# A fused attention and FFN kernel: the order of work from a table of places instead of shifts

## The chip, the core and the metric

One NeuronCore of a Trainium2 chip runs the kernel. Times are microseconds of device time of an execution; the median of the runs counts. The engines are TensorE (PE, matmuls; PEld is its weight load), VectorE (DVE), ScalarE (ACT), GpSimd (POOL), and SyncE (SP), which issues every DMA of this kernel.

## What is computed

Four batches of eight heads, 576 rows of 64 columns, go through causal attention and a memory retrieval, mixed by a gate; the result, as 2304 tokens of 512, goes through a feed-forward layer of 2048 with its own negative slope for each hidden unit:

```python
scores = scale * np.matmul(q, k.transpose(0, 1, 3, 2))
scores = np.where(causal, -1000000000.0, scores)
a = np.exp(scores - scores.max(-1, keepdims=True))
a /= a.sum(-1, keepdims=True) + 1e-09
local = np.matmul(a, v)
q_p = phi(q)                                   # elu(q) + 1
mem_out = einsum(q_p, M_prev) / (einsum(q_p, z_prev) + 1e-06)
x = g * mem_out + (1 - g) * local              # g = sigmoid(beta), per head
h = x @ w_in                                   # 2304 x 512 by 512 x 2048
y = (np.maximum(h, 0.0) + alpha * np.minimum(h, 0.0)) @ w_out
```

The two weight matrices arrive as 64-bit floats. The kernel reads them as pairs of 32-bit integers and puts fp32 together on DVE.

## The kernel before

The rows are cut so that each batch has 64 first rows and four blocks of 128. The 64 first rows of all four batches make a group of their own, `Z`, which comes first; then each batch goes in two halves (blocks 1 and 2, blocks 3 and 4), and each half is a group of 256 tokens for the feed-forward layer. Attention, the retrieval and the layer's two matmuls of different groups overlap.

The names that matter in the trace: `R` are the weights (and the first rows' k and v before them); `kn` and `E` also hold weight pieces at the start. `q`, `kn`, `vn` and `zb` are loads. `s`, `s2` are scores in PSUM, `P` the probabilities, `PT` the turned ones (a DMA turns them), `bank` the product of `PT` and `v`, `xn` the scaled result, `x` the turned `xn`. `h` is the layer's first product, `gg` its activated value in two fp16 parts, `y` the second product, `t` the rows to store. `qT`, `k` and `qS` (a copy of `qT` with its halves swapped) feed the scores. `gco`, `igc`, `iom` are made from beta, `oma`, `ast`, `scd` and `scr` from alpha.

Nothing of this is issued where it is written. Every call on an engine goes through `Work.add`, which records the operation, what it depends on and a price from `Work.price`. `Work.phase` names each one's stage: `LW0` to `LW3` are loads of weight pieces, `C0` to `C3` their conversion (`to_f32`, three DVE operations of 128x1024 for a piece, whose data come in two loads), `J` the small constants, `sZ` and `oZ` the first rows' scores and values, `s21`, `P21`, `o21` scores, probabilities and values of batch 2's first half, `h1_11` and `y1_11` the two products of batch 1's first group, its second four steps, and so on. At the end `Work.issue` puts all 6253 operations (4158 of PE, 1053 of DVE, 626 of ACT, 138 of POOL, 278 DMAs) into one order, and the engines run theirs in it; only data and buffers hold an instruction back. All of them stand in the trace under the line that issues them, L487.

`lay` makes the order: a list scheduler with one clock for each engine, that takes of the operations that are ready the one with the lowest rank. In the kernel before, ranks begin as latest start times. `STAGES` then shifts all operations of a stage, or of a stage on one engine, by one number, and passes forwards and backwards follow, stage after stage of the table:

```python
rank = [x + 1e3 * sum(bias.get(k, 0) for k in ...) for x, op in zip(rank, ops)]
start = self.lay(before, after, rank)
```

So two operations of one stage on one engine keep the distance that the latest start times gave them, unless `lay` itself parts them.

Of the kernel before, what the change touches and what calls it, by code (L numbers as in the profile page):

```python
# [31 lines left out]
STAGES = [  # L32
    (2, {
        "A0": 10.6, "A:DVE": 50.6, "BK0": 102.5, "BK:ACT": -27.7, "BK:PE": 3.4, "C0": -56.4, "C1": 22.3, "C2": 335.8,
        "C3": -920, "C:ACT": 1096.2, "C:DVE": -3.8, "C:PE": -943.6, "I": -699.2, "I:DVE": 79.2, "I:POOL": 497.7,
        "J:ACT": 470.6, "J:DVE": 108, "J:PE": -179.3, "K": 47.5, "K:POOL": 2.3, "L0K": -713.8, "L0K:DMA": 228.2,
# [6 lines left out]
        "LW:DMA": 605.3, "LZ": 27.3, "LZ:DMA": -1145.9, "Lz": 8.5, "Lz:DMA": -8.6, "N": 87.9, "N:PE": 292.5,  # L43
        "P01": 4, "P03": 3.7, "P11": 777.2, "P13": 823.4, "P21": 168.1, "P23": 236.6, "P31": -675.3, "P33": -247.2,
        "P:ACT": 988.7, "P:DMA": 668.5, "P:DVE": -882.6, "P:PE": -157.8, "S0": 4737.2, "S1": -1253, "S3": -2953.6,
        "S:ACT": -87.5, "S:DVE": 168.1, "V0": -874.8, "V:DVE": 211.2, "V:PE": -90.8, "a0": 5.7, "a1": 46.8,
        "a2": -161.5, "a3": 389.6, "a4": -42.9, "a:ACT": -265.2, "a:DVE": 239.4, "bk0": -173.5, "bk1": 344.8,
        "bk2": 244.5, "bk3": 3.1, "bk:ACT": -687.5, "bk:DMA": 246.9, "bk:DVE": 1380.7, "bk:PE": 100.3, "bv0": -0.7,
# [1479 lines left out]
```

## Time and profile before

| | us |
|---|---|
| median of 3 runs | 562.34 |
| the runs | 561.42 to 563.78 |
| the profiled execution | 563.66 |
| its span | 561.9 |

The span is what the views below divide; 1.76 us of the profiled execution lie outside it. Idle time in a view of one engine stands in brackets at the end of a row, with what released the engine. A DMA's row on SP is its issue, the landing comes later. PE's weight loads run beside its matmuls, and the start of one matmul to the start of the next, not its own duration, is what it costs.

### The profile page before, as it was taken

What the parts mean: (1) busy time and instruction counts of PE and PEld (TensorE: products, weight loads), DVE (VectorE), ACT (ScalarE), POOL (GpSimd) and SP (SyncE); (2) the same over time, 40 slices, a digit from 0 to 9 for tenths busy, and PEclk for the clock granted to TensorE, in tenths of its full rate; (3) what the DMA queues carried; (4) which work ended last, traced back from release to release, by engine and by line L of the source; (5) the groups of instructions that cost most, each with busy time, mean ns of one, the idle gap of its engine ahead of it and who ended that gap; (6) DMA issues with size and microseconds to landing.
All of it is one profiled execution on the core that took longest, in us unless ns stands there. A gap on an engine that the chain in (4) does not pass through costs nothing. (4 is left out here: it accounts for less than half of the span.)

```text
span 561.9 us, 11984 instructions
## 1 busy us (share of the span) xinstructions
PE 536.4 (95%) x4421; PEld 353.5 (63%) x4421; DVE 450.9 (80%) x1197; ACT 376.7 (67%) x790; POOL 82.8 (15%) x142
## 2 busy tenths in 40 slices
PE   9749999999999899999998999999999999999997
PEld 3448654556557566658555766578578765866663
DVE  4989999999999799999897999998679974233232
ACT  2568996778998369978785787796579873232222
POOL 3000510031220012221222110431112110000000
PEclk9869999999999999999998999999999999999999
DMA  8998595836359997579999816799446963000000
GB/s 283 239 353 202 155 238 173 244 94 153 89 127 184 214 231 170 101 140 210 194 201 198 175 34 146 160 232 178 58 118 111 167 138 88 12 11 2 37 1 37
DMA packets 226026, 82.84 MB, mean 147 GB/s; under 512 B 216224, under 2 KB 216240, under 8 KB 225968
## 3 DMA queue, kind: packets, MB, share of 16 engines
q1 hardware_dynamic: 225968, 82.09, 64.5%
q8 instruction: 34, 0.56, 0.4%
q14 instruction: 24, 0.20, 0.1%
HBM read 35.66 MB, written 5.77 MB: 74 GB/s over the span
## 5 line engine op out<-in xcount | busy, mean ns | idle before, releaser
L487 PE MATMUL h<-x,R 128*128 128x256 f16 x1536 | 246.7, 273 | 1.9 <-DMA x<-xn 1.4
L487 PE MATMUL y<-R,gg 128*128 128x512 f16 (+1 forms) x832 | 247.0, 399 | 0.8 <-ACT k L487 0.6
L487 PE MATMUL bank<-v,PT 128*128 128x64 f16 x1224 | 182.1, 193 | 5.3 <-DMA PT<-P 4.5
L487 PEld LDWEIGHTS <-R 128*128 128x128 f16 x1536 | 148.6, 98 | 36.9 <-issue 6.5
L487 PEld LDWEIGHTS <-gg 128*128 128x128 f16 x768 | 74.4, 98 | 78.3 <-DVE gg L487 1.8
L487 PEld LDWEIGHTS <-PT 128*128 128x128 f16 x1224 | 114.4, 98 | 13.6 <-DMA PT<-P 6.9
L487 POOL TENSOR_SCALAR E<-q,nrm,sm 128x64 f32<-128x64 f32 x112 | 67.9, 618 | 310.9 <-DVE sm L487 269.8
L487 ACT ACTIVATE E<-E,mx 128x320 f32<-128x320 f32 (+3 forms) x136 | 81.1, 602 | 21.5 <-DVE mx L487 17.4
L487 DVE SCALAR_TENSOR_TENSOR P<-E,mx,P 128x384 f16<-128x384 f32 (+2 forms) x112 | 75.3, 699 | 8.5 <-ACT P L487 8.4
L487 ACT ACTIVATE P<-E,mx 128x384 f16<-128x384 f32 (+2 forms) x112 | 71.0, 675 | 15.8 <-POOL E L487 12.0
L487 DVE SCALAR_TENSOR_TENSOR r<-r,oma,h 128x256 f32<-128x256 f32 x128 | 56.6, 475 | 20.2 <-ACT r L487 20.0
L487 DVE SCALAR_TENSOR_TENSOR gg<-r,gsc,gg 128x512 f16<-128x512 f32 x56 | 41.8, 748 | 36.5 <-ACT gg L487 35.0
L487 ACT ACTIVATE r<-h 128x512 f32<-128x512 f32 x72 | 42.3, 589 | 35.8 <-PE h L487 23.9
L487 ACT ACTIVATE gg<-r,gsc 128x512 f16<-128x512 f32 x56 | 40.1, 717 | 37.4 <-PE y L487 33.4
L487 DVE CUSTOM_DVE_ANT_0 E<-s,mask,pm 128x320 f32<-128x320 f32 (+2 forms) x96 | 56.9, 608 | 7.6 <-PE s L487 7.5
L487 PE MATMUL s<-k,qT 128*128 128x64 f16 (+5 forms) x136 | 37.9, 294 | 1.3 <-DMA k<-k 1.3
L487 PE MATMUL s<-k,qS 128*128 128x192 f16 (+4 forms) x120 | 34.0, 294 | 0.0
L487 PE MATMUL h<-R 128*128 128x256 f32 x128 | 32.7, 383 | 0.0
L487 PEld LDWEIGHTS h<-R 128*128 128x128 f32 x128 | 22.3, 192 | 6.6 <-issue 3.0
L487 ACT ACTIVATION_READ_ACCUMULATOR E<-E,mx 128x1 f32 x124 | 23.5, 189 | 0.0
L487 ACT ACTIVATE xn<-bank,xsc 128x256 f16<-128x256 f32 x28 | 12.9, 462 | 12.3 <-PE bank L487 12.3
L487 DVE SCALAR_TENSOR_TENSOR xn<-bank,xsc,xn 128x256 f16<-128x256 f32 x28 | 13.4, 480 | 9.4 <-ACT xn L487 9.4
(183 smaller groups left out, 636.7 us busy)
## 6 DMA issues: line engine op xcount, KB each, us to landing
q<-in_q_dram SPq DMA_DIRECT2D x16, 256.0 KB, 4.3
vn<-in_v_dram SPq DMA_DIRECT2D x16, 256.0 KB, 5.2
out_dram<-t SPq DMA_DIRECT2D x16, 256.0 KB, 2.4
kn<-in_moe_w_in_dram SPq DMA_DIRECT2D x6, 512.0 KB, 6.7
kn<-in_moe_w_out_dram SPq DMA_DIRECT2D x6, 512.0 KB, 5.3
kn<-in_k_dram SPq DMA_DIRECT2D x12, 256.0 KB, 4.0
qS<-qT SPq DMA_DIRECT2D x24, 128.0 KB, 2.6
R<-in_moe_w_in_dram SPq DMA_DIRECT2D x4, 512.0 KB, 5.6
```

The costliest lines, as they stand in the source:

```text
L487: fn(*a, **kw)
```

## The change

`STAGES`, with its passes and shifts, goes. `PLAN` takes its place: for each stage on each engine a string of steps, one for each operation (`*n` repeats one), whose running sum, times 100, is the rank of that operation. `issue` makes a single pass of `lay` with these ranks. The prices of DMAs in `price` change as well. Operations, their data, tiles, buffers and dependencies are the same in both kernels; the recording line moves from L487 to L750.

```diff
-STAGES = [
-    (2, {
-        "A0": 10.6, "A:DVE": 50.6, "BK0": 102.5, "BK:ACT": -27.7, "BK:PE": 3.4, "C0": -56.4, "C1": 22.3, "C2": 335.8,
...
+PLAN = {
+    "J:DVE": "-904 -12 133 -418 41 302 131 -23 130 -170 6 -430 573 -88",
+    "LW0:DMA": "-1100 449 -440 244 189 169 -485 666",
...
             if "transpose" in name:
-                return (800 + 1.75 * kb if kb > 400 else 1130 + 0.6 * kb), 190 + 3.45 * kb, 1655, -1
+                return (800 + 1.75 * kb, 4.1 * kb, 1700, -1) if kb > 400 else (1130 + 0.6 * kb, 3.78 * kb, 1885, -1)
...
             if run >= 4096:
-                return 400, (2.75 if self.phase in ("LW0", "LW1") else 4.9) * kb, 2000, packets
+                rate, late = {"LW0": (3.2, 2600), "LW1": (2.7, 2450)}.get(self.phase, (3.55, 2150))
+                return 400, rate * kb, late, packets
             if run >= 512:
-                return 540, max(300, 4.06 * kb), 1800, packets
-            return 620, (273 if kb > 200 else 200) + 4.17 * kb, 2100, packets
+                if o.tensor.name in self.fixed:
+                    return 400, 1.4 * kb, 1950, packets
+                return (560, 5.3 * kb, 1765, packets) if kb < 200 else (530, 4 * kb, 1800, packets)
+            return (600, 4.5 * kb, 2050, packets) if kb > 200 else (620, 6 * kb, 2090, packets)
...
-        rank = late
-        for passes, bias in STAGES:
-            rank = [x + 1e3 * sum(bias.get(k, 0) for k in dict.fromkeys((
...
+        plan = {}
+        for x, steps in PLAN.items():
+            at, ranks = 0, []
+            for step, _, times in (y.partition("*") for y in steps.split()):
+                for _ in range(int(times or 1)):
+                    at += int(step)
+                    ranks.append(100.0 * at)
+            plan[x] = iter(ranks)
+        start = self.lay(before, after, [next(plan[f"{op[7]}:{op[0]}"]) for op in ops])
```

What that does to the rows is seen at two places. The first is the start. SP's first rows before:

```order
L487 DMA R<-in_moe_w_in_dram 128x1024 x4
L487 DMA kn_90<-in_moe_w_in_dram 128x1024
L487 DMA xn_103<-in_moe_alpha_dram 16x128
L487 DMA q_1_94<-in_z_prev_dram 64x512 x4
L487 DMA kn_90<-in_moe_w_in_dram 128x1024
L487 DMA gco<-in_beta_dram 128x8
L487 DMA E_0_92<-in_moe_w_in_dram 128x1024 x2
L487 DMA q_0_93<-in_q_dram 64x8x64
```

and SP's first rows now:

```order
L750 DMA R<-in_moe_w_in_dram 128x1024 x2
L750 DMA E_0_92<-in_moe_w_in_dram 128x1024
L750 DMA R<-in_moe_w_in_dram 128x1024
L750 DMA kn_90<-in_moe_w_in_dram 128x1024
L750 DMA R<-in_moe_w_in_dram 128x1024
L750 DMA gco<-in_beta_dram 128x8
L750 DMA q_1_94<-in_z_prev_dram 64x512
L750 DMA kn_90<-in_moe_w_in_dram 128x1024
L750 DMA q_1_94<-in_z_prev_dram 64x512 x2
L750 DMA xn_103<-in_moe_alpha_dram 16x128
```

The two loads of a piece of weights stood next to one another for the first pieces; now the loads of four pieces are interleaved, gco is the seventh instead of the twelfth and alpha (to `xn`) the twelfth instead of the sixth. DVE's first conversions, in rows with the semaphores that they wait for (DMAHW0 to 7 go to the loads in turn, so that DMAHW1 and DMAHW3 are the second and the fourth), before:

```order
L487 TENSOR_SCALAR R<-R 128x1024 [waits DMAHW1_49,DMAHW0_49]
L487 SCALAR_TENSOR_TENSOR R<-R 128x1024 [waits DVE_49] x2
L487 TENSOR_SCALAR R<-R 128x1024 [waits DMAHW3_49,DMAHW2_49]
L487 SCALAR_TENSOR_TENSOR R<-R 128x1024 [waits DVE_49]
L487 TENSOR_REDUCE ast_89<-bank_67 128x1 [waits PE_49]
L487 TENSOR_SCALAR oma<-bank_67 128x16
L487 SCALAR_TENSOR_TENSOR R<-R 128x1024 [waits DVE_49]
```

and now:

```order
L750 TENSOR_SCALAR R<-R 128x1024 [waits DMAHW3_49,DMAHW1_49]
L750 SCALAR_TENSOR_TENSOR R<-R 128x1024 [waits DVE_49] x2
L750 TENSOR_SCALAR igc<-igc 128x8 [waits Activation_49]
L750 TENSOR_SCALAR R<-R 128x1024 [waits DMAHW5_49,DMAHW0_49]
L750 RECIPROCAL iom<-igc 128x8 [waits DVE_49]
L750 SCALAR_TENSOR_TENSOR R<-R 128x1024 [waits DVE_49]
L750 TENSOR_SCALAR iom<-iom 128x8 [waits DVE_49]
```

The first conversion waits for later loads than before, the chain from beta (igc, iom) stands between the first conversions, and that from alpha (ast, oma) comes after them.

The second place is where batch 1's layer and batch 2's attention overlap. SP's rows there, from the transposes of batch 1's last probabilities to those of batch 2's first (the first two `PT` that are 10 blocks wide), before:

```order
L487 DMA_TRANSPOSE PT_116<-P_100 128x18x128
L487 DMA qS<-qT 64x1024 x2
L487 DMA_TRANSPOSE k_65<-k_0_101 128x10x128
L487 DMA out_dram<-t_1_118 128x512
L487 DMA_TRANSPOSE PT_113<-P_99 128x18x128
L487 DMA_TRANSPOSE k_65<-k_1_102 128x10x128
L487 DMA_TRANSPOSE PT_114<-P_100 128x18x128
L487 DMA_TRANSPOSE x_111<-xn_104 128x4x128
L487 DMA q_1_94<-in_q_dram 128x8x64 x2
L487 DMA kn_90<-in_k_dram 128x8x64 x2
L487 DMA_TRANSPOSE PT_115<-P_99 128x10x128
L487 DMA_TRANSPOSE PT_116<-P_100 128x10x128
```

and now:

```order
L750 DMA qS<-qT 64x1024 x2
L750 DMA_TRANSPOSE x_111<-xn_103 128x4x128
L750 DMA_TRANSPOSE PT_116<-P_100 128x18x128
L750 DMA_TRANSPOSE k_65<-k_0_101 128x10x128
L750 DMA q_1_94<-in_q_dram 128x8x64 x2
L750 DMA_TRANSPOSE PT_113<-P_99 128x18x128
L750 DMA_TRANSPOSE PT_114<-P_100 128x18x128
L750 DMA kn_90<-in_k_dram 128x8x64 x2
L750 DMA_TRANSPOSE k_65<-k_1_102 128x10x128
L750 DMA_TRANSPOSE x_111<-xn_104 128x4x128
L750 DMA_TRANSPOSE PT_115<-P_99 128x10x128
L750 DMA_TRANSPOSE PT_116<-P_100 128x10x128
```

The copies to `qS` (and the store, which is now further ahead) come before the wide `PT_116`, the q loads before the wide `PT_113`, and a `k` and an `x` transpose stand where q and kn loads stood ahead of the narrow `PT_115`. PE's rows around the first matmul that reads this `PT_115`, before:

```order
L487 MATMUL h_123<-x_110,R 128x256
L487 LDWEIGHTS R
L487 MATMUL h_124<-x_111,R 128x256
L487 LDWEIGHTS PT_115
L487 MATMUL bank_67<-v_66,PT_115 128x64
L487 LDWEIGHTS R
L487 MATMUL h_124<-x_111,R 128x256
```

and now:

```order
L750 MATMUL h_123<-x_111,R 128x256
L750 LDWEIGHTS gg_150
L750 MATMUL y_131<-R,gg_150 128x512
L750 LDWEIGHTS PT_115
L750 MATMUL bank_67<-v_66,PT_115 128x64
L750 LDWEIGHTS gg_150
L750 MATMUL y_131<-R,gg_150 128x512
```

The matmuls of the group on `x_110` are all done by then in the new order, and the `h` and `y` of the next group, on `x_111`, stand further on.

## Rows read from the trace of the kernel before

**Rows 1.** The page, busy time, share and instructions of each engine.

```profile
PE 536.4 (95%) x4421; PEld 353.5 (63%) x4421; DVE 450.9 (80%) x1197; ACT 376.7 (67%) x790; POOL 82.8 (15%) x142
```

**Rows 2.** Stretches: length, busy time by engine, granted clock (PEclk), DMA share, GB/s.

```profile
20.00:40.00 20.00, 9.98 (x84) 7.54 (x85) 18.17 (x79) 13.96 (x48) 0.00 (x0) 0.69 1.15 304
47.00:299.00 252.00, 244.99 (x1902) 158.14 (x1901) 240.77 (x641) 200.37 (x417) 45.69 (x71) 1.00 0.76 175
299.00:303.00 4.00, 1.35 (x15) 0.98 (x13) 2.16 (x6) 1.60 (x4) 1.69 (x2) 1.00 0.97 129
303.00:310.00 7.00, 7.00 (x49) 4.15 (x48) 5.35 (x15) 4.05 (x10) 0.77 (x2) 0.76 0.93 199
310.00:470.00 160.00, 159.41 (x1549) 110.34 (x1547) 138.16 (x375) 122.45 (x259) 30.36 (x54) 1.00 0.68 137
470.00:556.00 86.00, 86.00 (x670) 57.62 (x669) 27.21 (x53) 23.69 (x37) 0.00 (x0) 1.00 0.05 16
```

**Rows 3.** Timeline of PE: start, duration, operation, [idle before <- releaser].

```profile
39.43 1.51 PE L487 MATMUL h<-ident,P 128*128 128x128 f32 x6 [2.83 <-DVE P L487]
```

**Rows 4.** Timeline of DVE, 6 to 36 us.

```profile
6.12 0.69 DVE L487 TENSOR_SCALAR R<-R 128x1024 int32<-128x1024 int32 x1 [5.00 <-DMA R<-in_moe_w_in_dram]
6.85 2.49 DVE L487 SCALAR_TENSOR_TENSOR R<-R 128x1024 int32<-128x1024 int32 x2
...
11.81 0.18 DVE L487 TENSOR_REDUCE ast<-bank 128x1 f32<-128x16 f32 x1 [0.54 <-PE bank L487]
...
15.14 0.16 DVE L487 TENSOR_SCALAR scr<-bank 128x1 int32<-128x1 int32 x1 [0.58 <-PE bank L487]
...
29.24 0.23 DVE L487 CUSTOM_DVE_ANT_0 P<-s,mz 128x64 f32<-128x64 f32 x1 [0.77 <-PE s L487]
...
35.80 0.16 DVE L487 TENSOR_SCALAR scr<-bank 128x2 int32<-128x2 int32 x1 [0.68 <-PE bank L487]
```

**Rows 5.** Timeline of SP's queue, the twelfth load and the two behind it.

```profile
9.23 0.33 SPq L487 DMA_DIRECT2D gco<-in_beta_dram  x1
11.22 0.80 SPq L487 DMA_DIRECT2D E<-in_moe_w_in_dram  x2
```

**Rows 6.** Timeline of PE, 298 to 308 us.

```profile
298.54 1.58 PE L487 MATMUL h<-x,R 128*128 128x256 f16 x13
302.77 0.20 PE L487 MATMUL bank<-v,PT 128*128 128x64 f16 x1 [2.65 <-DMA PT<-P]
...
303.34 0.38 PE L487 MATMUL y<-R,gg 128*128 128x512 f16 x1
303.55 0.27 PE L487 MATMUL h<-x,R 128*128 128x256 f16 x1
...
308.10 0.40 PE L487 MATMUL bank<-v,PT 128*128 128x64 f16 x8
```

**Rows 7.** Timeline of SP's queue, 278 to 302 us.

```profile
278.29 2.06 SPq L487 DMA_TRANSPOSE PT<-P  x1
280.45 1.17 SPq L487 DMA_DIRECT2D qS<-qT  x2
...
283.12 0.58 SPq L487 DMA_DIRECT2D out_dram<-t  x1
...
292.94 1.16 SPq L487 DMA_DIRECT2D q<-in_q_dram  x2
...
296.32 5.59 SPq L487 DMA_TRANSPOSE PT<-P  x2
```

**Rows 8.** Timeline of PE, the smaller waits that the text names.

```profile
233.65 0.19 PE L487 MATMUL bank<-v,PT 128*128 128x64 f16 x1 [0.77 <-DVE xn L487]
...
266.87 0.20 PE L487 MATMUL bank<-v,PT 128*128 128x64 f16 x1 [0.28 <-DMA PT<-P]
...
282.25 0.20 PE L487 MATMUL bank<-v,PT 128*128 128x64 f16 x1 [1.06 <-DMA PT<-P]
...
453.72 0.28 PE L487 MATMUL h<-x,R 128*128 128x256 f16 x1 [0.35 <-DVE r L487]
```

More of the change, by code (lines that the diff above doesn't have):

```diff
@@ L29 @@
 PN = [1, 1, 1, 1, 1]
-STAGES = [
-    (2, {
-        "A0": 10.6, "A:DVE": 50.6, "BK0": 102.5, "BK:ACT": -27.7, "BK:PE": 3.4, "C0": -56.4, "C1": 22.3, "C2": 335.8,
-        "C3": -920, "C:ACT": 1096.2, "C:DVE": -3.8, "C:PE": -943.6, "I": -699.2, "I:DVE": 79.2, "I:POOL": 497.7,
-        "J:ACT": 470.6, "J:DVE": 108, "J:PE": -179.3, "K": 47.5, "K:POOL": 2.3, "L0K": -713.8, "L0K:DMA": 228.2,
[6 rows of a table removed]
[L43 to L48, printed above, removed]
[5 rows of a table removed]
-        "o31": 144.8, "o33": 10.1, "o:ACT": -779.8, "o:DMA": 580.1, "o:DVE": -613.6, "o:PE": 33.3, "oZ": 10.8,
[5 rows of a table removed]
-        "v:DVE": 634.9, "v:PE": 331.4, "x0": -121.5, "x:ACT": 2.1, "x:DVE": 73.7, "y0_10": -412.5, "y0_11": -68.6,
-        "y0_30": 187.3, "y0_31": 1834.4, "y1_10": -18.1, "y1_11": 103.3, "y1_30": -419.6, "y1_31": 103.8,
-        "y2_10": 184.2, "y2_11": 220.2, "y2_30": -3073.8, "y2_31": -122.6, "y3_10": 764.1, "y3_11": 98,
-        "y3_31": 447.3, "y4_11": -1599.1, "y:ACT": -1231.1, "y:DMA": 642.8, "y:DVE": -750.7, "y:PE": 1282.7,
-    }),
[4 rows of a table removed]
-        "C3:PE": -8.9, "C:ACT": 13.2, "C:DVE": 9.3, "C:PE": -17.2, "I": -57.9, "I:POOL": -8.6, "J:ACT": -18.7,
[6 rows of a table removed]
-        "LW3": -8.7, "LW3:DMA": -22.1, "LW:DMA": -2.8, "LZ:DMA": -42.6, "Lz:DMA": -4.4, "N": 0.9, "N:PE": -13.7,
[5 rows of a table removed]
-        "P33:DMA": -3.8, "P33:DVE": -7.4, "P33:POOL": -37, "P:ACT": 15, "P:DMA": -20.1, "P:DVE": 8.9, "P:PE": -86.4,
[21 rows of a table removed]
-        "h4_11:PE": -16.7, "h:ACT": 10, "h:DVE": 8.9, "h:PE": -16.3, "n": -27.5, "n:PE": -9.4, "o01": -15,
[5 rows of a table removed]
-        "o33:DVE": 21.3, "o33:PE": -55.2, "o:ACT": -0.5, "o:DMA": -50.1, "o:DVE": 13.1, "o:PE": -18, "oZ": -97,
[4 rows of a table removed]
-        "q:ACT": 39, "q:DVE": 9.7, "r0:ACT": 0.9, "r0:DVE": 9.9, "r:ACT": 35.7, "r:DVE": 13.6, "s01:ACT": -1.2,
[4 rows of a table removed]
-        "s33:ACT": 1.7, "s33:PE": -49.1, "s:ACT": 12.1, "s:DVE": 8.9, "s:PE": -16.3, "sZ": 8.1, "sZ:ACT": 98.3,
[14 rows of a table removed]
-        "y4_11:PE": -16, "y:ACT": 21.9, "y:DMA": 2.5, "y:DVE": 8.4, "y:PE": -16.3,
-    }),
[4 rows of a table removed]
-        "C3:PE": -26.7, "C:ACT": 47.4, "C:DVE": -22.5, "C:PE": 1, "I:DVE": -32.9, "I:POOL": 4.3, "J": 37.8,
[13 rows of a table removed]
-        "P33:DMA": -13.2, "P33:DVE": -9.1, "P:DMA": -3.5, "P:DVE": -22.3, "P:PE": 0.2, "P:POOL": -11, "S0": 2.9,
[27 rows of a table removed]
-        "o33:PE": 65.8, "o:ACT": 7.4, "o:DMA": -10.7, "o:DVE": -24.8, "o:PE": 144.2, "oZ": -53.6, "oZ:ACT": 8.9,
[9 rows of a table removed]
-        "s33:DVE": -8.2, "s33:PE": 41.6, "s:ACT": -5, "s:DVE": -22.3, "s:PE": 143.8, "sZ": -0.9, "sZ:ACT": 37.5,
[15 rows of a table removed]
-        "y:PE": 143.8,
-    }),
-]
@@ L212 @@
+PLAN = {
[447 rows of a table added]
+}
 WINDOW = 3413.0
@@ L465, in issue @@
                 after[d].append((i, lag))
-        late = [0.0] * len(ops)
-        hold = [max(op[5], op[8][0]) for op in ops]
-        pe = 0.0
-        for i in reversed(range(len(ops))):
-            took = ops[i][8][0] + ops[i][8][1] if ops[i][0] == "DMA" else hold[i]
-            late[i] = min([late[f] - lag for f, lag in after[i]], default=0.0) - took
-            if ops[i][6]:
-                late[i] = pe = min(late[i], pe - hold[i])
-        rank = late
-        for passes, bias in STAGES:
-            rank = [x + 1e3 * sum(bias.get(k, 0) for k in dict.fromkeys((
-                op[7], op[7].rstrip("0123456789_") + ":" + op[0], op[7] + ":" + op[0]))) for x, op in zip(rank, ops)]
-            for n in range(passes):
-                if n:
-                    back = self.lay(after, before, [-s - h for s, h in zip(start, hold)], True)
-                    rank = [-s - h for s, h in zip(back, hold)]
-                start = self.lay(before, after, rank)
-            rank = start
+        plan = {}
[7 more added lines that the diff above has]
+        start = self.lay(before, after, [next(plan[f"{op[7]}:{op[0]}"]) for op in ops])
         with tc.manual_schedule():
```

2 lines of the change are left out of this document (1 added, 1 removed), and 592 rows, old and new, of tables (PLAN, STAGES).

## The prediction

> **What bounds the kernel now.** I read the engine totals first: PE is busy 95% of the span, DVE 80% [rows 1]. Then the stretches [rows 2]. In 20:40 DVE works 18.17 of 20 us, while PE has 9.98 us of work at a granted clock of 0.69 (1.00 is the level of 2.4 GHz, 0.5 that of 1.2 GHz). In 47:299 both are nearly full: PE 244.99 and DVE 240.77 of 252, the clock at 1.00. Then one hole: PE works 1.35 of 4 us in 299:303, and the clock is 0.76 for the 7 us behind it. After that PE is full (159.41 of 160, 86.00 of 86). So there are two regimes. Up to about 40 us what counts is when DVE ends the first rows' attention: PE's h transposes of P wait 2.83 us for it, until 39.43 [rows 3]. After 47 us it is PE's own work plus the waits in it. The same instructions run in both kernels, so an order can only change waits, stretches at the lower clock and changes between kinds of matmul. The waits after 47 us are 7.01 (47:299), 2.65 and 0.59 (310:470): **10.2 us in all** [rows 2], beside some 1.7 us lost at the lower clock. That is the purse of the second regime. As DVE is nearly as full as PE in 47:299, a late start isn't made good there by DVE.
>
> **Part 1, the start.** DVE's first conversion of a weight piece starts at 6.12, after 5.00 us of waiting for loads, and from there DVE is nearly unbroken [rows 4]. In the new order the queue of loads begins with one load each of two pieces, and the first conversion waits for the second and the fourth load. When did the fourth land? SP has eight loads in flight and issues the next when the oldest has landed: the twelfth load's issue at 9.23, that of gco, waited for the fourth landing [rows 5]. So the first conversion starts at about 9.25: **+3.1 us**. Against it stand DVE's waits in its chain of small constants in the old order: three for PE's bank between 11.8 and 15.2 (0.54, 0.71, 0.58; the first and the last are shown), 0.77 for s, 0.68 for the bank again [rows 4]: **−3.3**. The new order puts that chain behind more conversions and lays reductions into the gaps, so I let these go. It has new waits of its own: the operation on igc, from beta's load gco, stands right behind the first piece, where DVE is at 9.25 + 3.2 = 12.5 (0.69 and 2.49 us of work [rows 4]); gco is now seventh, behind six loads of 512 KB. The fourth and the fifth landed 2.0 us apart, since E's issue at 11.22 waited for the fifth [rows 5]; one more at that step is at 13.2, and the small load comes right behind it: 0.9 us of wait with ACT's operation between. The turned alpha, loaded later than before, I price the same. So **+1.8**, and the sum is **+1.6 us**. Bounds: 0, if DVE's new waits hide under one another and under reductions; +4.9 (3.1 + 1.8), if none of the old waits goes. I take +1.6, nearer to the lower bound, since the operations with the old waits [rows 4] do move behind longer work. What is late here is late at the end, as PE's first h transposes wait for it already [rows 3].
>
> **Part 2, the hole at 300 us.** The bank matmul at 302.77 stands idle for 2.65 us, released by a DMA that turns P (PT<-P) [rows 6]. That transpose was issued at 296.32, behind two q loads (1.16 us) and two kn loads, in a queue that runs back to back from 278 on [rows 7]. Two things change. On PE more h and y matmuls of batch 1's last groups stand ahead of this bank: counted from the program's start, with 0.11 us for an h (13 in 1.58) and 0.22 for a y (303.34 to 303.55, from a y to the h behind it) [rows 6], 286.4 us of other matmuls instead of 281.6, so **4.8 us more cover**. And in the queue the q loads move ahead of older transposes, so that fewer loads stand right ahead of this one. The producer of P has 0.36 us more DVE work ahead. With 4.8 against 2.65 + 0.36 the wait goes: **−2.65 us**. With it goes the lower clock behind it: 7.00 us of busy PE at 0.76 [rows 2] would be 5.3 at 1.00, **−1.7 us**. Bounds: −4.35 as it stands; 0, if the queue hands PE's later arrival a later transpose. I take the whole gain, the cover being nearly twice the hole.
>
> **Part 3, the smaller waits.** By the same count (work ahead of the waiting matmul, work ahead of its producer, place in the queue): two waits for PT of 0.28, the first at 266.87, and 0.35 for r at 453.72 go, **−0.9**. At 233.65 (0.77 for xn) DVE has more work ahead: **+0.6**. At 282.25 (1.06 for PT) an out store and two qS copies, 0.58 and 1.17 us of the queue [rows 7], now stand ahead of the transpose that was issued at 278.29, while PE has 1.4 us more work ahead: **+0.4** [rows 8]. The other waits keep their place in the queue and about their work ahead; I leave them, at −0.4 to +0.4 in sum.
>
> **Part 4, what brings next to nothing.** A matmul on 64 or fewer rows beside one on all rows costs a small step. There are 96 such changes in the old order and 91 in the new, but four of the five that go lie ahead of 47 us, where PE waits anyway: 0. The tail from 470 us, where PE alone is full [rows 2], has the same matmuls in nearly the same order: 0. In 390:440 the second half of batch 3's attention comes 4 to 11 us earlier, but PE has only 0.59 us of waits to give back in 310:470: 0 beyond the 0.35 above. The new prices of DMAs and the single planning pass act when the program is built, and not on the chip: 0.
> Matmuls of 64 columns next to one another rise from 106 pairs to 119. Eight of them from 308.10 take 0.40 with 0.20 for the single one at 302.77 [rows 6], so (0.40 − 0.20) / 7 = 0.03 us each: 13 more of these pairs cost nothing beyond the work itself. The Trainium skill ("TensorE: Matmul & The Clock Gate", "Back-to-back issue gap") says that in a stream of weight loads and matmuls both set the spacing, about 81 ns for 128 columns; by that, an estimate, 13 pairs would cost 13 × 51 ns = 0.7 us more. The trace disagrees with this rule, and I go by the row.
>
> **Sum.** +1.6 − 2.65 − 1.7 − 0.9 + 0.6 + 0.4 = −2.65, say −2.7 us. The profiled execution took 563.66 with a span of 561.9, 1.3 above the median of 562.34 and within the runs shown; so a profiled run would take 561.0, and the median becomes **559.6**.
>
> **The rivals.**
> *More holes close than my count can see.* If the start costs nothing (0 instead of +1.6), and of the 10.2 us of waits, of which I remove 3.6, half of the other 6.6 go as well (−3.3), the time is 559.6 − 1.6 − 3.3 = 554.7. For it: the waits of 47:299 are short ones, mostly for DMAs behind loads, and the loads are spread anew. Against it: DVE is as full as PE there, which leaves an order little to trade.
> *The cover is only borrowed.* The 4.8 us of matmuls put ahead of the bank at 302.77 are taken from behind it, where they covered the next transposes; the 2.65 come back as several short waits, with the clock at 1.00. Then 559.6 + 2.65 = 562.2, no change. For it: the queue is full [rows 7], so later transposes don't come earlier.
> *SP's queue becomes the bound, slower than before.* Three transfers (1.75 us) now stand ahead of the transpose of 282.25, and two q loads ahead of the next. If PE's extra work doesn't cover them, the 1.06 becomes 2.8, with the lower clock behind it, 1.7 us as at 302.77; and the queue, having no gap, hands its lateness on, so that the 4.35 of part 2 isn't won: 559.6 + (1.75 − 0.4) + 1.7 + 4.35 = 567.0. It decides from where that wait reaches the 2.65 us of the one hole after 47 us behind which the clock fell. Against it: the transfers that move ahead leave from behind, so that the queue's sum is the same by 300.
> *The order stays as it was* is excluded: the order emitted differs, as the rows above show.
>
> **How the numbers follow.** Forecast, 559.6 with ±1.5 for the start's bounds: 0.40. More holes, 554.7: 0.25. Borrowed cover, 562.2: 0.21. Queue, 567.0: 0.14. About 0.5%, 2.8 us, is what a measurement of this kernel can tell from no change: under 559.5 is faster, over 565.2 slower. The forecast lies on that edge, and 0.19 of its 0.40 falls below. Faster 0.25 + 0.19 = 0.44; same 0.21 + 0.21 = 0.42; slower 0.14. The range reaches from a little under the middle of the first rival, 554.3, to 565.0; it leaves out the queue's case and the far part of the first rival, 0.2 in all.
>
> **What would show it.** DVE's first conversion at 9.2 instead of 6.12, and the h transposes of P at 41 instead of 39.43 (at 39.5 or before, part 1's +1.6 is wrong; at 44 its upper bound holds). No PE wait over 1 us in 290:320 and a clock of 1.00 from 47 to 556: part 2. No waits where 266.87 and 453.72 stood, and 1 to 1.5 us for the bank near 282: part 3. I am wrong if a hole over 2.5 us stands anywhere after 47 us, or if PE's waits there still sum to 10 us.

## The result

The new order is slower: 568.89 us (median of 4 runs, 567.13 to 571.29) against 562.12 for the kernel before on the same chip. The ratio is 1.011, with a 95% interval of 1.0081 to 1.0139. The forecast was 559.6, with a range that ended at 565.0, and slower by more than 0.5% had a chance of 0.14.

The profiled execution is the longest of the four, 571.29 us with a span of 569.4. Its page, by busy time and instructions of each engine, answers to [rows 1]:

```profile
PE 537.1 (94%) x4421; PEld 354.7 (62%) x4421; DVE 452.1 (79%) x1197; ACT 379.3 (67%) x790; POOL 79.9 (14%) x142
```

Same instructions, same busy time: everything was lost in waits and in stretches at the lower clock. The stretches of the new kernel (length, then PE, PEld, DVE, ACT, POOL busy, granted clock, DMA share, GB/s) say where; 47:299 and 470:556 answer to [rows 2]:

```profile
20.00:40.00 20.00, 7.88 (x87) 6.37 (x87) 18.42 (x80) 15.21 (x50) 0.00 (x0) 0.66 1.07 246
40.00:50.00 10.00, 8.83 (x80) 7.36 (x80) 10.00 (x15) 3.88 (x7) 0.00 (x0) 0.50 1.01 291
47.00:299.00 252.00, 241.84 (x1849) 156.47 (x1846) 235.94 (x618) 195.68 (x401) 43.19 (x66) 0.99 0.75 171
140.00:220.00 80.00, 73.09 (x628) 48.49 (x627) 71.97 (x174) 58.88 (x108) 10.24 (x14) 0.98 0.75 158
300.00:320.00 20.00, 17.52 (x160) 11.41 (x159) 17.25 (x55) 15.42 (x38) 5.40 (x9) 0.91 0.96 184
470.00:556.00 86.00, 86.00 (x672) 58.20 (x670) 28.05 (x57) 25.80 (x40) 0.76 (x2) 1.00 0.11 30
```

and three of the same stretches in the kernel before:

```profile
40.00:50.00 10.00, 9.96 (x98) 8.50 (x97) 10.00 (x11) 6.94 (x13) 0.00 (x0) 0.77 0.94 208
140.00:220.00 80.00, 76.86 (x643) 50.13 (x642) 75.82 (x185) 61.70 (x115) 11.29 (x16) 1.00 0.76 169
300.00:320.00 20.00, 17.35 (x133) 12.18 (x132) 15.48 (x41) 11.82 (x28) 3.76 (x6) 0.91 0.97 205
```

In 40:50 the new kernel runs at the lower level throughout (0.50 against 0.77) and PE has a gap more. In 140:220 PE waits 6.9 us instead of 3.1. In 300:320, where the old hole stood, PE waits as long as before (2.5 against 2.6 us), at the same clock.

Windows on the clock compare different work. So I also took both traces operation by operation: each of PE's 4158 operations got the shorter of its two start-to-start times as its work, and at equal work done I read off how far the new kernel is behind:

| time in the kernel before | 50 | 100 | 162 | 172 | 183 | 196 | 206 | 247 | 257 | 303 | 314 | 445 | 556 |
|---|---|---|---|---|---|---|---|---|---|---|---|---|---|
| new kernel behind by, us | 3.9 | 3.9 | 4.4 | 4.2 | 7.4 | 8.2 | 9.8 | 8.6 | 10.3 | 6.4 | 8.6 | 8.1 | 7.6 |

This is the most useful reading of the case: two steps up (by 50 us, and between 172 and 206) and a smaller one at 250. From 257 on the distance falls to 6.4 at 303, most of it while the kernel before stands in its own hole of 2.65 us [rows 6], is back at 8.6 by 314, after the new kernel's hole there, and ends at 7.6. (The two profiled executions are 1.5 and 2.4 us above the medians of their kernels, so the difference of the traces is 0.8 larger than that of the medians.) PE's waits behind it, from the timeline of PE in the new kernel:

```profile
41.17 0.88 PE L750 MATMUL h<-ident,P 128*128 128x128 f32 x3 [2.92 <-DVE P L750]
...
180.22 0.55 PE L750 MATMUL bank<-v,PT 128*128 128x64 f16 x13 [2.04 <-DMA PT<-P]
...
184.77 0.38 PE L750 MATMUL y<-R,gg 128*128 128x512 f16 x1 [0.67 <-DVE t L750]
...
203.47 0.33 PE L750 MATMUL s<-k,qT 128*128 128x192 f16 x2 [2.57 <-DMA k<-k]
...
259.77 0.20 PE L750 MATMUL bank<-v,PT 128*128 128x64 f16 x1 [1.52 <-DMA PT<-P]
...
304.48 0.39 PE L750 MATMUL y<-R,gg 128*128 128x512 f16 x1 [0.52 <-ACT gg L750]
...
312.83 0.24 PE L750 MATMUL s<-k,qT 128*128 128x192 f16 x1 [1.96 <-DVE mx L750]
```

Both signs of being wrong that the forecast names are there: a hole over 2.5 us (2.57 at 203.47), and waits that sum to 10 us, since 47:299 alone has 10.2 (252 less 241.84), where the kernel before has 7.0. The first row answers to [rows 3], 1.74 us later. The two at 304 and 312 stand where [rows 6] had one wait of 2.65 for PT: that one is gone, and a wait for mx, the row maxima from DVE, has nearly its length. And DVE's start, which answers to [rows 4]:

```profile
9.27 0.69 DVE L750 TENSOR_SCALAR R<-R 128x1024 int32<-128x1024 int32 x1 [8.15 <-DMA R<-in_moe_w_in_dram]
...
13.27 0.17 DVE L750 TENSOR_SCALAR igc<-igc 128x8 f32<-128x8 f32 x1 [0.79 <-ACT igc L750]
...
18.08 0.17 DVE L750 TENSOR_SCALAR oma<-bank 128x16 f32<-128x16 f32 x1 [0.82 <-PE bank L750]
...
30.61 0.23 DVE L750 CUSTOM_DVE_ANT_0 P<-s,mz 128x64 f32<-128x64 f32 x1 [1.14 <-PE s L750]
```

The granted clock of each run, averaged over its span, goes with the time: the four runs of the new kernel took 571.29 us at 0.973, 569.76 at 0.976, 568.03 at 0.979 and 567.13 at 0.982. The profiled execution of the kernel before has 0.982 as well and took 563.66, so most of the loss is there without the clock too.

### The profile page after: what moved, and what is told of

Its sections match the earlier page's. It is cut to its first block, busy times and chain, and to the rows that moved or that the text cites. A ratio compares the mean times of both kernels' runs of the same rounds, so it can differ in the third digit from the quotient of the medians.

```text
span 569.4 us, 11962 instructions
## 1 busy us (share of the span) xinstructions
PE 537.1 (94%) x4421; PEld 354.7 (62%) x4421; DVE 452.1 (79%) x1197; ACT 379.3 (67%) x790; POOL 79.9 (14%) x142
## 4 chain that ended last, share of the span: by engine, by line
PE 69%; DVE 12%; DMA 8%; ACT 4%; issue 2%; SPq 2%; POOL 1%; POOLq 0%; ACTq 0%; DVEq 0%
PE y L750 28%; PE h L750 27%; PE s L750 7%; PE bank L750 5%; DMA PT<-P 3%; DVE P L750 2%; SPq L750 2%; DMA q<-in_z_prev_dram 2%; DVE R L750 2%; POOL E L750 1%; DVE E L750 1%; DMA k<-k 1%; DVE r L750 1%; PE bank L581 1%; DVE gg L750 1%
## 5 line engine op out<-in xcount | busy, mean ns | idle before, releaser
L750 PE MATMUL y<-R,gg 128*128 128x512 f16 (+1 forms) x832 | 253.6, 399 | 1.4 <-DVE t L750 0.9
L750 PE MATMUL h<-x,R 128*128 128x256 f16 x1536 | 250.3, 274 | 1.0 <-DVE r L750 0.5
L750 PE MATMUL bank<-v,PT 128*128 128x64 f16 x1224 | 180.5, 193 | 3.6 <-DMA PT<-P 3.6
L750 PEld LDWEIGHTS <-R 128*128 128x128 f16 x1536 | 149.5, 98 | 33.2 <-DVE r L750 3.7
L750 PEld LDWEIGHTS <-gg 128*128 128x128 f16 x768 | 74.5, 98 | 78.6 <-issue 2.7
L750 PEld LDWEIGHTS <-PT 128*128 128x128 f16 x1224 | 113.7, 98 | 13.0 <-issue 5.1
L750 POOL TENSOR_SCALAR E<-q,nrm,sm 128x64 f32<-128x64 f32 x112 | 63.9, 582 | 318.8 <-DVE sm L750 270.8
L750 ACT ACTIVATE E<-E,mx 128x320 f32<-128x320 f32 (+3 forms) x136 | 81.0, 601 | 21.8 <-DVE mx L750 19.8
L750 DVE SCALAR_TENSOR_TENSOR P<-E,mx,P 128x640 f16<-128x640 f32 (+3 forms) x112 | 75.7, 698 | 9.5 <-ACT P L750 9.1
L750 ACT ACTIVATE P<-E,mx 128x640 f16<-128x640 f32 (+3 forms) x112 | 71.1, 673 | 15.6 <-POOL E L750 10.7
L750 DVE SCALAR_TENSOR_TENSOR r<-r,oma,h 128x256 f32<-128x256 f32 x128 | 56.7, 473 | 29.9 <-ACT r L750 29.8
L750 ACT ACTIVATE r<-h 128x512 f32<-128x512 f32 x72 | 42.1, 590 | 42.0 <-PE h L750 27.3
L750 DVE SCALAR_TENSOR_TENSOR gg<-r,gsc,gg 128x512 f16<-128x512 f32 x56 | 41.7, 746 | 33.1 <-ACT gg L750 23.6
L750 ACT ACTIVATE gg<-r,gsc 128x512 f16<-128x512 f32 x56 | 40.0, 717 | 32.2 <-PE y L750 27.1
L750 DVE CUSTOM_DVE_ANT_0 E<-s,mask,pm 128x576 f32<-128x576 f32 (+3 forms) x96 | 56.7, 607 | 1.0 <-PE s L750 0.7
L750 PE MATMUL s<-k,qT 128*128 128x512 f16 (+5 forms) x136 | 38.2, 298 | 4.6 <-DMA k<-k 2.6
L750 PE MATMUL s<-k,qS 128*128 128x192 f16 (+4 forms) x120 | 34.0, 300 | 0.0
L750 PE MATMUL h<-R 128*128 128x256 f32 x128 | 32.0, 384 | 0.2 <-ACT R L750 0.2
L750 PEld LDWEIGHTS h<-R 128*128 128x128 f32 x128 | 22.8, 192 | 6.6 <-issue 2.7
L750 ACT ACTIVATION_READ_ACCUMULATOR E<-E,mx 128x1 f32 x124 | 23.4, 189 | 0.0
L750 ACT ACTIVATE t<-y,u 128x512 f32<-128x512 f32 x18 | 12.3, 683 | 16.1 <-PE y L750 15.5
L750 ACT ACTIVATE R<-R,wsc 128x1024 f16<-128x1024 f32 x16 | 18.3, 1142 | 4.8 <-DVE R L750 4.8
```

The source lines that it names most:

```text
L750: fn(*a, **kw)
```

## The experiments

All of them issue the same 6253 operations; only the list of the order differs, and each list is built from the old one and the new one:

```diff
-            for i in sorted(range(len(ops)), key=lambda i: (start[i], i)):
+            for i in order:
```

The first so many operations of both orders are nearly the same set (up to operation 1075, for one, they differ in 3), so an order can be cut there and go on with the other one. `rest(x)` below stands for the operations of order x that are not issued yet. Each comparison has its own runs of the kernel before, whose median is given beside it.

### Which stretch loses

```diff
+ e1_old_start:   order = before[:350] + rest(after)
+ e2_new_start:   order = after[:350] + rest(before)
+ e3_new_middle:  order = before[:1075] + rest(after[:2150]) + rest(before)
+ e4_old_middle:  order = after[:1075] + rest(before[:2150]) + rest(after)
```

> The first 350 operations (up to about 46 us) go in the order of the kernel before, all others in the new order. In the profiled executions the new order's PE is 3.6 to 4.0 us behind the old one at 50 us of the program (1.74 of it when the h transposes of P start), 9.75 behind at 205, 7.6 at the end. Theory (the loss is made in two places, start and 139 to 226 us, each by itself): 568.9 - 4.0 = 565. Rival 1 (only the start is wrong, and the holes after 139 us are its late arrival handed down): 560 to 562. Rival 2 (of the start only the 1.74 belongs to the order, the rest is the clock's chance in one execution): 567.

> The first 350 operations in the new order, all others in the order of the kernel before. Theory: 562.1 + 4.0 = 566. Rival 1 (a late start makes holes later): 569 or more. Rival 2: 563.8.

> Operations 1 to 1075 and from 2151 on in the order of the kernel before; those between (about 139 to 226 us) in the new order. Theory: the middle by itself costs what PE loses there in the profile, 9.75 - 4.05 = 5.7 us, so 567.8. Rival 1 (the middle is only hit because the start is late): 562 to 563.

> The new order throughout, but operations 1076 to 2150 (about 139 to 226 us) in the order of the kernel before. Theory: 568.9 - 5.7 = 563.2. Rival 1 (the middle's holes come from the late start, whatever the order there): 568 to 569.

Measured, beside 561.54: e1 566.68 (ratio 1.0090, 1.0069 to 1.0111), e2 566.45 (1.0094, 1.0070 to 1.0119), e3 565.22 (1.0068, 1.0040 to 1.0095), e4 565.49 (1.0069, 1.0048 to 1.0090).

So the start alone costs +4.9 us and the middle alone +3.7, as the cuts have them. Rival 1, the late start that makes the later holes, falls: with the old start the middle still loses (e1, e3), and with the old middle behind the new start nothing is lost there (in e2's trace PE is 3.2 us behind at 162 and 3.3 at 206). Rival 2 falls too: the start costs more than its 1.74.

A part of the 4.9 belongs to the cut and not to the new start. At operation 350 the two orders meet so that ACT squares two converted pieces of weights ahead of its copies to `R` that the first `h` matmuls read; in each whole order it squares one. PE waits for these copies in e1 and e2 (and in f3 and h4 below), and in neither whole kernel, e1 first, then e2:

```profile
48.54 1.78 PE L894 MATMUL h<-R 128*128 128x256 f32 x7 [1.27 <-ACT R L894]
```

```profile
50.77 1.56 PE L894 MATMUL h<-R 128*128 128x256 f32 x6 [1.23 <-ACT R L894]
```

Without it the start costs about 3.7 us (4.9 − 1.2), an estimate from e2 and this row. From the other side each part seems to give back less: the new order costs 6.8 beside its own runs of the kernel before, e1 5.1 and e4 3.9, so that 1.6 (2.9 with the wait of 1.27 taken out) come back for the start and 2.8 for the middle. Against 3.7 and 3.7 that isn't a difference these intervals can show. In e1's trace PE also falls 1.6 behind in the stretch that holds the wait for PT at 259, which none of these cuts takes alone. And in e2's trace 1.5 of the 3.2 us come back behind 303: the wait at the place of the old hole is 2.12 us instead of 2.65, and the lower clock behind it isn't there. 140:220 and 300:320 of e2 read

```profile
140.00:220.00 80.00, 76.86 (x648) 50.47 (x644) 75.83 (x178) 62.38 (x115) 12.03 (x18) 1.00 0.78 171
300.00:320.00 20.00, 17.88 (x167) 13.52 (x164) 17.38 (x49) 13.89 (x33) 4.88 (x8) 1.00 1.07 203
```

with the clock at 1.00 in the second, against 0.91 in both kernels above.

### Engines or queue in the middle

```diff
+ f1_mid_queue:   PE, DVE, ACT, POOL as in before; SP's DMAs as in e3
+ f2_mid_engines: PE, DVE, ACT, POOL as in e3; SP's DMAs as in before
```

> The order of the kernel before on PE, DVE, ACT and POOL; only SP's queue of DMAs between operations 1076 and 2150 (139 to 226 us) has the new order. The new middle with its queue took 565.2 beside 561.5 of the kernel before. Theory Q (SP's queue makes the middle's holes: in the trace of the new order the k transpose is issued 9.5 us after its data, behind stores and other transposes): 565. Rival E (the engines' order makes the data late and the queue only follows): 561.5.

> The new order on PE, DVE, ACT and POOL between operations 1076 and 2150, but SP's queue as in the kernel before; everything else as before. Theory Q: 561.5 to 562. Rival E: 565 or more.

Measured, beside 562.10: f1 564.52 (1.0044, 1.0017 to 1.0071), f2 574.03 (1.0234, 1.0172 to 1.0295). The queue's order by itself costs 2.4 us, nearer to theory Q (3.5 over the kernel before) than to rival E (nothing). But the old queue under the new engines costs 12. Neither E nor Q says that: the two orders belong together, and a queue that doesn't follow its producers makes the longest hole of all these traces, PE of f2:

```profile
224.35 0.23 PE L888 MATMUL bank<-v,PT 128*128 128x64 f16 x1 [7.77 <-DMA PT<-P]
```

In f1 one can see how two places in a full queue work. SP's queue in f1, where x<-xn now stands behind a reload of a part (the first half of a group's `y`, which was stored and is read back into `t`), a store and a qS copy:

```profile
182.92 0.54 SPq L888 DMA_DIRECT2D t<-part  x1
183.51 0.50 SPq L888 DMA_DIRECT2D out_dram<-t  x1
184.07 0.58 SPq L888 DMA_DIRECT2D qS<-qT  x1
184.75 1.26 SPq L888 DMA_TRANSPOSE x<-xn  x1
```

and in the kernel before, where it was issued at

```profile
183.47 1.26 SPq L487 DMA_TRANSPOSE x<-xn  x1
```

1.3 us of issue became 2.4 of waiting, PE of f1 against PE of the kernel before:

```profile
188.25 2.08 PE L888 MATMUL h<-x,R 128*128 128x256 f16 x9 [3.60 <-DMA x<-xn]
```

```profile
185.86 0.38 PE L487 MATMUL h<-x,R 128*128 128x256 f16 x2 [1.21 <-DMA x<-xn]
```

But these 2.4 us are no share of the 3.7 that the new middle costs. In e3, where the engines have the new order too, the same matmul waits 0.28 for x, and other waits have grown:

```profile
174.01 0.55 PE L896 MATMUL bank<-v,PT 128*128 128x64 f16 x13 [1.65 <-DMA PT<-P]
188.66 1.58 PE L896 MATMUL h<-x,R 128*128 128x256 f16 x13 [0.28 <-DMA x<-xn]
197.33 0.33 PE L896 MATMUL s<-k,qT 128*128 128x192 f16 x2 [1.78 <-DMA k<-k]
```

Of these f1 has only the first, with 0.23 us (at 173.88), as the kernel before.

### Moving single transposes

```diff
+ g1_mid_x_first:   as e3; in SP's queue the second x<-xn of o03 three places ahead
+ g3_old_x_k_first: as before; in SP's queue that x<-xn two places and the first k<-k of batch 1 six places ahead
```

> The old order with the new middle (operations 1076 to 2150; 565.2 in that form beside 561.5 of the kernel before), and in SP's queue one DMA moved: the second x transpose of o03 goes ahead of a part's reload, a store and a qS copy that the new queue has ahead of it. In the trace of that form it was issued 2.2 us after its data and PE's h waited 2.5 us for it. Theory (the place of single transposes in SP's queue makes the holes): 1.8 us of the wait go, 563.4. Rival (PE then waits as long for the next DMA of the full queue): 565.

> The order of the kernel before with two DMAs moved in SP's queue and nothing else: the second x transpose of o03 goes two places ahead, before the qS copies, and the first k transpose of batch 1 (issued at 191.15 with its data ready at 183.79) seven places ahead. Theory (SP's queue holds these two and PE waits 1.21 and 0.94 us for them): 2 us less than the kernel before. Rival (the queue is full there, what is pushed back makes PE wait as long): no difference.

Measured, beside 561.65: g1 563.50 (1.0040, 1.0018 to 1.0063), g3 561.68 (0.9992, 0.9974 to 1.0010). In g3's order k stands six places further ahead, and not seven as expected. g3 settles it for the old order: no difference. The waits for x and k shrank or went, and PE waited for the next thing, a reload that was pushed back and so t on DVE. PE of g3:

```profile
185.19 3.11 PE L888 MATMUL h<-x,R 128*128 128x256 f16 x27 [0.59 <-DMA x<-xn]
189.61 0.38 PE L888 MATMUL y<-R,gg 128*128 128x512 f16 x1 [1.31 <-DVE t L888]
```

g1's median is 1.8 us nearer to its kernel before than e3's, as the theory has it, but the intervals overlap, and in its trace PE loses as much in the middle as in e3's (3.4 us in both); its wait for y<-R,gg is now 1.94:

```profile
189.35 0.38 PE L888 MATMUL y<-R,gg 128*128 128x512 f16 x1 [1.94 <-DVE t L888]
```

So g1 leaves it open: its median is the theory's 563.4, and its trace looks like the rival's.

### Another queue

```diff
+                if i in (1428, 1430, 1431, 1433, 1435, 1436, 1814, 1818):
+                    fn = tc.nc.gpsimd.dma_start
```

This goes into the old order (h1), into e3 (h2) and into the late cut that comes below (h3): four reloads of parts and four stores of the middle are issued from POOL. On the page of h1 these eight stand in a queue of another kind (`software_dynamic`, 512 packets), so the issuing engine isn't all that changes.

> The order of the kernel before, with eight DMAs of batch 4's and batch 0's y groups in the middle (four reloads of parts, four stores) issued from POOL instead of SP; nothing else. They take 0.54 to 0.6 us each of SP's queue between 174 and 197 us. Theory Q (SP's one queue is full there, and what stands in it delays the x and k transposes): PE's waits of 1.21 (x) and 0.94 (k) go, 560. Rival T (the transfers and their data, not the queue, set the times): 561.7.

> The old order with the new middle (565.2 in that form), with the same eight DMAs issued from POOL. Theory Q (the new middle loses by what its order puts into SP's full queue ahead of x, the reloads and k): most of the 3.4 us that PE loses there comes back, 562. Rival T (DVE and PE themselves are later in the new middle): 565.

> The old order up to operation 2650 and the new one behind it (560.8, the fastest form so far), with the same eight DMAs issued from POOL. Theory Q: 559. Rival T: 560.8.

Measured, beside 562.11: h1 561.94 (0.9987, 0.9956 to 1.0018), h2 563.82 (1.0028, 1.0005 to 1.0051), h3 560.37 (0.9975, 0.9949 to 1.0000). Theory Q falls for the old order: SP issues the k transposes 3 us earlier, and PE waits for them no less. SP's queue of the kernel before and of h1:

```profile
191.15 3.14 SPq L487 DMA_TRANSPOSE k<-k  x2
```

```profile
188.17 4.97 SPq L890 DMA_TRANSPOSE k<-k  x2
```

and PE of h1, where the kernel before had 0.94 at 195.26:

```profile
196.07 0.33 PE L890 MATMUL s<-k,qT 128*128 128x192 f16 x2 [1.33 <-DMA k<-k]
```

From issue to landing a `k` transpose in this stretch took longer, in the kernel before and in h1:

```profile
DMA to landing us min/median/max: 3.9/4.1/4.6
```

```profile
DMA to landing us min/median/max: 3.0/6.5/7.9
```

So what was gained at the issue was lost on the way to the landing. That the same transfers beside it hold the transpose up, whichever engine issued them, fits these rows, but isn't isolated: in g3, where k moved ahead of them in SP's own queue, PE's wait for k was gone. The Trainium skill says ("DMA: Bandwidth & Descriptors", "Issuing engines are not separate DMA queues"): DMAs of all issuing engines run on the same DMA engines, and issuing from several saves only issue time. These runs agree: 561.94 beside 562.11 us. In the new middle h2 costs 1.7 us, e3 3.7, with intervals that overlap; so at most a part of its loss is issue time. h3 lies 0.4 from rival T.

### The middle cut in two

```diff
+ k2_mid_first_half: order = before[:1075] + rest(after[:1525]) + rest(before)
+ k3_old_to_176:     order = before[:1525] + rest(after)
```

> The order of the kernel before, with the new order only for operations 1076 to 1525 (139 to 176 us), the first third of the middle (565.2 with all of it, 561.5 to 562.1 without). In the traces with the new middle PE falls 2.7 of its 3.4 us behind where it waits for the first PT of o03's second half and then for a reload, at 174 to 180 us. Theory H (the data of that PT are made later, because 1.6 us more of other DVE work stand ahead, and that is the middle's loss): 564.5. Rival W (the loss belongs to the queue behind it, with x, reloads and k): 562.

> The order of the kernel before up to operation 1525 (176 us), the new order behind it: old start, old first third of the middle, the rest new. The new order from 261 us on gained 1.3. Theory H: 561 to 561.5. Rival W: 563.5 to 564.

Measured, beside 562.21: k2 562.64 (1.0012, 0.9988 to 1.0035), k3 562.98 (1.0015, 0.9993 to 1.0037). The part to 176 us costs 0.4 us, within what can be told from nothing, although its wait for PT stands there in full (1.79 us at 175.08 in k2's trace): behind it the old order has its own waits, and takes a part of a delay up. k3 has everything new from 176 on and costs 0.8, while the part from 261 on gains 1.3 (below); so 176 to 261 costs about 2.1. Theory H (564.5 and 561 to 561.5) falls, and W (562 and 563.5 to 564) is off by about 0.6 in each. By the medians the two parts together, 2.5, cost less than e3's 3.7 for a shorter stretch; with intervals of more than 1 us to each side that difference isn't shown.

### The late part, and a version that beats both

```diff
+ f4_new_late:  order = before[:2650] + rest(after)
+ g2_new_later: order = before[:2775] + rest(after)
```

> The order of the kernel before up to operation 2650 (about 261 us), the new order behind it. In the traces with the new order PE comes 0.9 to 1.9 us nearer to the old one between there and the end. Theory (the late part of the table is a gain by itself): 559.6 to 560.7. Rival (it only gets back what the earlier part lost, by covering a late queue): 561.5.

> The order of the kernel before up to operation 2775 (about 269 us), the new order behind it; with the change at operation 2650 it took 560.8 beside 562.1, and its PE waited 1.3 us for a PT at 266 that the old order has without a wait of more than 0.3. Theory (that hole is the new order's own, the gain lies behind it): 559.5. Rival (the gain needs the stretch with that hole): 561 to 562.

Measured: f4 560.81 beside 562.10 (0.9976, 0.9960 to 0.9992), g2 560.89 beside 561.65 (0.9988, 0.9974 to 1.0001). The late part of the table is a gain by itself, 1.3 us, small, but its interval leaves out 1. f4 beats both kernels; h3, its form with another queue, has the same ratio. In g2 the gain isn't shown: the interval holds 1. So the rival that the stretch with the wait at 266 is needed isn't refuted, nor is the theory borne out. f4 in 300:320, and PE's waits there:

```profile
300.00:320.00 20.00, 19.15 (x170) 13.39 (x170) 17.86 (x49) 17.16 (x38) 3.64 (x6) 1.00 0.95 219
```

```profile
300.02 0.27 PE L888 MATMUL h<-x,R 128*128 128x256 f16 x1 [1.53 <-DMA x<-xn]
303.53 0.24 PE L888 MATMUL s<-k,qT 128*128 128x192 f16 x1 [0.73 <-DVE mx L888]
```

The hole of 2.65 for PT has become two of 1.53 and 0.73 for other things, 2.26 in sum. The clock is 1.00 instead of 0.91, but that isn't shown to be the late order's gain. g3 has the old order there and a longer hole at the same matmul than the kernel before, and its clock stays at 1.00, PE and 300:320 of g3:

```profile
302.29 0.20 PE L888 MATMUL bank<-v,PT 128*128 128x64 f16 x1 [2.75 <-DMA PT<-P]
```

```profile
300.00:320.00 20.00, 17.71 (x155) 13.37 (x156) 16.84 (x46) 13.58 (x32) 3.40 (x6) 1.00 0.97 208
```

So it is in e2, e3, f1 and g1, with holes of 2.12 to 2.29 us at this matmul, while h2 (2.48) and k2 (2.10) have 0.91 like the kernel before. The lower clock behind this hole comes in some executions and not in others; what makes up the 1.3 us of f4 stays open. f4 also has a wait of 1.28 for a PT at 266.63, where the kernel before has 0.28 and the new kernel none: that one the cut makes.

### The start taken apart

```diff
+ f3_whole_pieces: as e2; SP's first six loads 299 300 297 298 311 305 instead of 297 299 311 300 305 298
+ h4_gco_third:    as f3; gco's load third instead of seventh
+ k1_new_whole:    as after; SP's first six loads as in f3
```

> The new order in the first 350 operations, the old one behind (566.4 in that form), but the first six loads in whole pieces: the two of the piece that DVE converts first, then the two of the second, then one each of the others. The first conversion should start at 6.1 instead of 9.2. Theory L (the late first conversion is what the new start costs, as the prediction put it): 3 us less, 563.4. Rival B (DVE catches up with the loads of the third and fourth piece, which come no earlier, and waits there instead): 565.5 to 566.4.

> The new start with whole pieces first (563.9, old order behind the start), and beta's small load gco third instead of seventh. DVE waited 3.18 us for igc in that form. Theory (the small load's place is the rest of what the new start costs): the second conversion starts at 9.4 instead of 12.65, the third at 14.3 with its own load instead of 15.9: 1.6 us less, 562.3. Rival (the fourth piece and the first rows' q and k, which land no earlier, bind anyway): 563.9.

> The new order throughout (568.9) but for the first six loads, which go in whole pieces. With the old order behind the start this gave back 2.5 us (566.4 to 563.9). Theory (the start's loss is handed through to the end, whatever follows): 566.4. Rival (the new order's later holes take the earlier start up): 568.9.

Measured: f3 563.93 beside 562.10 (1.0036, 1.0007 to 1.0065), h4 564.85 beside 562.11 (1.0053, 1.0029 to 1.0076), k1 567.77 beside 562.21 (1.0091, 1.0053 to 1.0129). With whole pieces the start costs 1.8 instead of 4.9 us; the intervals of f3 and e2 just meet (1.0065 and 1.0070). Theory L's 563.4 is near, but its 3 us of DVE time did not come as such, and 0.8 of the 3.1 us between e2 and f3 are the cut's: PE's wait for ACT's copies to `R` is 0.45 us in f3 and 1.23 in e2 (1.50 in h4). DVE of f3 starts at 6.17 and then waits 3.18 for beta's constants, where e2 waited 0.94:

```profile
6.17 0.69 DVE L888 TENSOR_SCALAR R<-R 128x1024 int32<-128x1024 int32 x1 [5.05 <-DMA R<-in_moe_w_in_dram]
...
12.57 0.17 DVE L888 TENSOR_SCALAR igc<-igc 128x8 f32<-128x8 f32 x1 [3.18 <-ACT igc L888]
```

With gco third that wait goes, and two others take its place; there is no gain over f3, as h4's rival has it. PE's h transposes of P start at 41.01, in f3 at 39.92. DVE of h4:

```profile
14.76 0.69 DVE L888 TENSOR_SCALAR R<-kn 128x1024 int32<-128x1024 int32 x1 [2.02 <-DMA kn<-in_moe_w_in_dram]
...
17.94 0.17 DVE L888 TENSOR_SCALAR oma<-bank 128x16 f32<-128x16 f32 x1 [2.49 <-PE bank L888]
```

In these traces DVE waits for loads at one place or the next; what the order of the small ones gives at the first it takes at the second. In the whole new order the repair gives 1.2 us (k1 costs 5.6, the new kernel 6.8, intervals overlapping), so the theory that the start's gain is handed through whole is not borne out, and its rival, that nothing is, isn't either.

The granted clock tells the starts apart. Averaged over the runs that its median is taken from, every form with the new start has 0.976 to 0.978 (the new kernel, e2, e4, f3, h4, k1); every form with the old start has 0.981 to 0.985 but f2, with its long holes, 0.974. A difference of 0.006 in 563 us is some 7 us more at the lower level, an estimate, and up to half of that in PE's time.

## Why the prediction was wrong

**What bounds the kernel: right.** PE's busy time didn't move (536.4 and 537.1), the tail in 470:556 is full in both, and all that changed is waits and clock. The purse of 10.2 us in waits after 47 us was read rightly. That the change could also put more into it, I weighed at one place only.

**Part 1, the start: right in mechanism, short in size.** DVE's first conversion at 9.27 (forecast 9.25), the two new waits of 0.79 and 0.82 (forecast 0.9 each), and P's h transposes at 41.17 (forecast 41) came as written. The wait for s did not go but grew, from 0.77 to 1.14. By the runs the start costs about 3.7 us (e2 without the cut's own wait) and not 1.6. The step that failed is the sentence that what is late there is late at the end, as if by the same amount. PE comes out of the start at its lower clock, at a time when it is already the bound. In the profiled execution it stayed there from 41.17 to about 50 (0.50 in all of 40:50), in the kernel before from 39.43 to about 45 (0.77). Those 9 and 5.5 us at half speed differ by (9 − 5.5) / 2 = 1.7 us, beside the 1.74. The term was missing from my sum. How long PE stayed at the lower clock differs between executions (40:50 has 0.71 in e2, whose first 350 operations are the same), but the forms with the new start have the lower clock on average in every case, 0.976 to 0.978 against 0.981 to 0.985.

**Part 2, the hole at 300 us: the wait named went, the gain didn't come.** The 2.65 for PT is gone, as the 4.8 us of cover said. But PE waits 1.96 for mx at 312.83, with the lower clock behind it, so that 300:320 has the same clock, 0.91, as before. My −4.35 stands against a measured −1.3 for everything from 261 us on (f4). This is close to the second rival, the borrowed cover: I counted what stands ahead of one matmul, and not what the same matmuls no longer cover elsewhere. By the two orders, the matmul that waits at 312.83, batch 2's scores, has lost 44 h and 21 y that stood ahead of it. And the −1.7 was no property of the order: I priced the clock of one execution. g3 has the hole with 2.75 us and the clock at 1.00 behind it, and e1 and k1 have the new order's wait for mx (1.82 and 1.69) with 1.00 in 300:320.

**Part 3: the step that failed.** "The other waits keep their place in the queue and about their work ahead; I leave them, at −0.4 to +0.4 in sum." They lost 3.7 us between 139 and 226 (e3) and more up to 261. Three waits that I priced at nothing grew: PT at 180.22 has 2.04, which was 0.21; k<-k at 203.47 has 2.57, which was 0.94; and t, at 184.77, is new with 0.67. The kernel before had

```profile
173.87 0.20 PE L487 MATMUL bank<-v,PT 128*128 128x64 f16 x1 [0.21 <-DMA PT<-P]
195.26 0.33 PE L487 MATMUL s<-k,qT 128*128 128x192 f16 x2 [0.94 <-DMA k<-k]
```

With the wait for x, which fell from 1.21 to 0.24, and one of a score matmul for mx, which rose from 0.46 to 0.99, PE's waits between 139 and 226 went from 2.8 to 6.5, and that is the 3.7.
"About their work ahead" was wrong for the largest. The PT of 180.22 has the same place in SP's queue in both orders and PE 0.2 us more work ahead, but DVE has three more operations ahead of its P (one each of `q1`, `h4_11` and `P03`), 1.3 us by their starts in the trace. The PT of 259.77 is alike: the same place, 0.3 us more on PE, and 1.9 us more on DVE (two of `p2`, one of `h0_31`). k2 has the first of these waits in full, 1.79, and costs only 0.4 us, so such a wait isn't lost whole where the waits behind it are the old ones.
"Their place in the queue" I had looked at in numbers of DMAs (the k transpose went from the 124th to the 125th), and waits one at a time. h1, g1 and g3 show that in this stretch they are not single: an earlier x is paid with a later t (g1, g3), and in k3, where PT doesn't wait, x's 1.21 became 0.20 and k's 0.94 became 2.53. f1 shows that the queue's order alone, with all engines as before, costs 2.4 us, by a reload and a copy that went ahead of x, but with the new engines that wait is gone, and f2, the other half, loses far more. What each change is worth within the 3.7 us therefore stays open.
Of the small terms, the −0.9 came: the waits of [rows 8] at 266.87 and 453.72 and their like are gone. The +0.6 and +0.4 did not: the waits of 0.77 and 1.06 went as well. In their place stand the 1.52 for a PT at 259.77, where the old order had no wait, and 0.52 for r at 289.62.

**Part 4: right as far as the traces show.** The tail is full in both; bank after bank is 0.03 us from start to start in the new kernel as in the old one.

**The rivals.** The slower one had the right sign and a time of 567.0, 1.9 under the measured one, partly by luck: it put the loss at 282, in SP's queue, and there the wait went. The loss was in the start, at 180 to 206, and at 259, in part by DVE's order. Its chance of 0.14 was low, because I looked for the danger at one place, and priced the many waits of 0.2 to 1.2 us elsewhere at nothing.
